# A refitted issue order and a refitted choice of masked tiles in an attention and FFN kernel

## The chip, the cores and the metric

The kernel runs on one core of a Trainium2 chip. A core has engines that run side by side, each with its own queue that it works off strictly in order: PE (matrix multiplication) with its weight loads (PEld), DVE (vector), ACT (activation), POOL (general), and SP, which here only issues transfers (DMA). The metric is the device time of one launch in microseconds. The kernel before takes 446.1 us, the median of three runs (445.67 to 448.51).

## The reference

Attention with a threshold, for 8 batches, 8 heads, 576 rows and a head size of 64, and after it an FFN over 4608 tokens with three parallel hidden layers (512 to 768) of which the largest value counts:

```python
scores = scale * np.matmul(q, k.transpose(0, 1, 3, 2))
thresh = np.max(scores, axis=-1, keepdims=True) - tau
scores = np.where(scores >= thresh, scores, -1e9)
attn = np.exp(scores - np.max(scores, axis=-1, keepdims=True))
attn = attn / (np.sum(attn, axis=-1, keepdims=True) + 1e-09)
x = np.matmul(attn, v)            # then heads side by side: 4608 x 512
h = np.maximum(np.maximum(x @ w1, x @ w2), x @ w3)
out = h @ w_out                   # 4608 x 512, float32
```

## The kernel before

A batch has two groups of four heads. Each group is nine chunks of 128 score rows; a chunk holds rows of two head pairs, r = 0 and 1, so a chunk has two score tiles of 128 x 576, 288 tiles in all. The last batch is done in two parts (four and five chunks for each group) so that its FFN can begin earlier.

The order of everything is written out by hand in one long string, ORDER. A loop at the end of the kernel reads it letter by letter, and each letter issues one step for the next item of its kind. Each engine is wrapped in `_Ordered`, which fixes its instructions in the order of the string, so the string decides the sequence in all queues. What one engine waits for from another follows from the data. Letters S, T, O and F carry a digit, the one of the four banks of PSUM that the step writes. A bank is free again when the engine that reads it is done.

The letters, by the engine that does the work:

- PE: S scores of a tile; T transposes q or k of a later group; O product of probabilities and v; F first half of an FFN product (hidden layer, tile ph, or output, tile po); B its second half.
- DVE: m the row maximum of a tile; k masks and sums a tile; r the reciprocals of a chunk's two sums; c copies transposed k; v maximum over the hidden layers (tiles hm, hT); w copies an attention output.
- ACT: e the first activation of a tile; n the second exponential with its sum; a copies transposed q; h copies the first hidden layer; x copies an attention output; u copies an FFN output.
- POOL: p scales a tile by its reciprocal (tile P); q swaps the halves of q (tile qs); y casts v; z casts weights.
- SP: l loads q, k and v of a later group; g loads weights (tile stage, 512 KB each); t transposes a chunk's P by DMA into ptq, which O reads; o stores results.

MASKED is a string of 288 bits, one for each score tile, and chooses between two ways to do its softmax. An unmasked tile (0) has its maximum on DVE, and then two activations on ACT: one that flattens all that lies below the threshold, and an exponential that sums (e and n). A masked tile (1) has its maximum on DVE, one exponential on ACT (e), and the threshold and the sum on DVE (k). So the bit moves work between ACT and DVE:

```python
def numerators(g, idx, r, zn, sm):
    acc = sm[:, r:r + 1]
    if masked(g, idx, r):
        vector.scalar_tensor_tensor(out=zn, in0=zn, scalar=thr, in1=zn,
                                    op0=OP.is_ge, op1=OP.mult, accum_out=acc)
    else:
        scalar.activation(out=zn, in_=zn, func=AF.Exp, scale=-1.0 / FLAT, accum_out=acc)
```

Buffers bind the engines to one another: four banks of PSUM, z tiles for four chunks, six P tiles, two stage tiles, two ptq. A prologue written as code (`beginning`) does the first group's q and k and the first two score tiles ahead of the string. Nearly all instructions are recorded at one line, that of the wrapper, so the profile is read by tile names.

Of the kernel before, what the change touches and what calls it, by code (L numbers as in the profile page):

```python
# [45 lines left out]
1eplBrkepF2tnmF3BnpvBnqvT1S0hprrcT2S3pamS1eymzF2emBeqgkF0etyS3nS1vpnmtF2pBmezBveS3prgnS0mtS1phrmT3epO2metzeF
0wpnS1gcqS2nmBqnmO3zekepgS1xvlF2nS3mtnF0rrmpBeBlpveS1lphS2mntF3zmeBrpS0evS1lpnmF2lnpS3rmleBptmS1nzvS0nS3mtpn
S2rpeF1rmepmtepS0mBepmtekF3ektekT2uBarklpukS0uqlS2urS1mlnS3pmleO0pmlepmelO2wtnkS1xrS0tepmF2myF3eBkepT1tBhcF0
nqvT2T1laByrcynS3qvS2nlqmF1tnpF0meS3pBelmBlhrrF2kpelS1vnBlprF3mnlS0pveBtprmS1hS2pmeS3tpmeS0pmF2emF1eBkeT3Bva
tF0nvqT2T3BkqlaS1nrcS3phmtS2npmF0epF1mteBqkBeqF3lnvS2lnBrvplS0hmtpS1F3meS2mteBrmepS0vnpO1rekpnO3mtnpweS2yrrt  # L50
xS1mF0yymT3epBcnS1pvS2nptF3meS0pmeBomT2hS1okeF0omF3ntBkaBervS1ponrF2vpemS0ptuS3mpeF2metknT1T3rknBparrceS0puS
3mqtuS1mpeS2mpeS3lmF0peomepS1ketqT3S2ncBqnmlqnmlO3ekluktO1urnwperrS0pxS3mptnS2mS1pempS3etmF0peF2meBlkBelS1kh
oF3nrmlF0pnBtvpBerrvS2phlS1mnpS3tmF0peS2mpeBmeF3vF1eoBkntS0vnBS2rmhpS3mepS1mteyF2mF0eyBkteBnrvT3pF1aovT2ynBp
lrcS3hplS0mnyF2lmF1elBykepBlnvT3tS0aS2vnO3rrmtpnmpeS1weptS2mS0prmO3eqtmeqF1eqlT0S2xqcBnlpmS3hlpS0meF2ymF1elB
knlF3vnBokBetS2hvS0nrrF3mpF1mpeBkBpetF2vnprS0uvnT3ptmS2aS1pmeS0trmF3epmnpkeS2tS0ermpBnmopnkS1uS2rurompS0eF3o
mpelmpeS2lkpeS0lmS1elqBmelqmetkO2unktO0erwpurkpT1txT2cS3apF0nmtT1qS2ceBqmnS1yF3hmF2eyrBpeBvptnF0pS1vnBrmtpS3
hS2pmeS0mtS1eF3meF2meBkBeF0knF1vnBBrvhpS3nvT0pF2akyF1tnBmyS0velByrmlS3phS2rlempF1lmyeF0pklBepS3tnvS2nBrmptO1
meprvepS2wnS3plmF0nF1rmepBlkeqS2lBhmtT3nyS0vnS2mqlO1emtpecT2xT0rS3pacF1eqmF2lnyBklqeT0BvlaS3khoS1qnmF0tF2pme
BrBopnvS3teprvF0pnrmS1puS2meS3prmS0epF1tmepmepT2ktBeqncT3tuS0kaS2urqmS3tnpmS1nF0pmemteS3repS1mS2lepmBelykteS
3kuO1rumplnmlpO0ewterpT2xS1cqnoS3mpF0nF2metBkeBkF1hlF3nvBlnrrS0pvlnBpmS2lhS1ymleF0mtS3epBmepF2vF1etkBnS0vnS3  # L60
rmBnpS2rhmpF0emF1pteBkpBerF3vnS2ptvnT0pBramS1pthS0mepF3meqtT2rBecpS1nvylT0ynS2pmlS3amlS1eomS0elO2rmpeomeplO3
ketnwT1F0nctF2xkBnBrvpS1hrF3pmS0qBemqS2onvF1yeF0mBopkeF3tyBnS2vqhBrlrnmpT1S0vaptS2empF1S3mpelBkeplF0vntS2rum
S1pnS0mtepF3rmepmetqS2kS0epBnmmteS1rkepS2lmuS0ulpmS1nlymT3yetF2cekeT3oBrknpamoS0npS3mnS1qtmuO0qurrmqelO2wpel
kpelS0xS3meptF2mS1peBemytF0hrkT3pBecF2nS1vpnS3rymtBpnmS0epS1vlnF3mF2etBmeBkhF0lkeF3nBrvpS1nrvBpnS2mptS0hmpeS
3meF2tmF1eBkeBlrvnT0plS3ravlpS2nlmqF0nlS1mqeBtrrmpF2eS3phBlmepS0tvepS1mS2npS3mepO0meknO1meownT3orxkT2pS0tacF
# [687 lines left out]
```

## Time and profile before

| | |
|---|---|
| median of 3 runs | 446.1 us (445.67 to 448.51) |
| the profiled execution | 446.82 us, span 445.0 us |
| PE busy | 423.6 us (95%) |
| ACT busy | 394.4 us (89%) |
| DVE busy | 393.2 us (88%) |
| POOL busy | 315.9 us (71%) |
| mean granted PE clock | 0.992 of full speed |

The span is the time from the first to the last instruction; the run's time has 1.8 us more around it. A share of busy time is a mean over the whole span, and the stages differ: the first FFN work can begin only when a batch's attention is done, and the last batch's FFN is left alone at the end. Matmuls are pipelined and their ends are modelled, so PE's gaps are seen better in the waits of its weight loads.

### The profile page before, as it was taken

The page shows a single profiled execution, that of the slowest core. Times are in us where ns is not written, and L with a number is a line of the kernel's source. Part 1 is how long each engine was busy: PE and PEld are TensorE (multiplying, and loading weights), DVE is VectorE, ACT ScalarE, POOL GpSimd, SP SyncE. Part 2 cuts the span into 40 slices and gives each one's busy share as a digit, 9 for nine tenths or more (in the row PEclk, how much of TensorE's full clock was granted, in tenths as well). Part 3 has the DMA queues.
Part 4 walks back from the last instruction along what each step waited for, and adds up shares of the span by engine and source line. Part 5 has one row for each costly group of instructions (what it writes and reads, how often), then busy time and mean ns, then how long its engine had stood idle before and what let it go on. Part 6 is the DMA issues. An engine that isn't in the chain of part 4 may idle for free.

```text
span 445.0 us, 14089 instructions
## 1 busy us (share of the span) xinstructions
PE 423.6 (95%) x5193; PEld 313.3 (70%) x5193; DVE 393.2 (88%) x1093; ACT 394.4 (89%) x804; POOL 315.9 (71%) x422
## 2 busy tenths in 40 slices
PE   7767799999999999999999999999999999999995
...
ACT  4999999999999999999998999999999999956422
...
GB/s 251 331 162 213 243 195 234 221 245 229 215 255 195 250 165 175 234 187 228 179 223 170 200 224 182 211 234 199 197 220 202 253 121 173 148 122 34 217 13 108
DMA packets 212773, 87.44 MB, mean 196 GB/s; under 512 B 185824, under 2 KB 199648, under 8 KB 212704
## 3 DMA queue, kind: packets, MB, share of 16 engines
...
q8 instruction: 41, 0.67, 0.6%
...
## 4 chain that ended last, share of the span: by engine, by line
PE 81%; ACT 7%; DVE 6%; issue 4%; POOL 2%; DMA 1%; DVEq 0%; POOLq 0%; ACTq 0%
PE ph L91 30%; PE sc L91 28%; PE po L91 11%; PE o L91 8%; ACT z L91 6%; PE tp L91 4%; DVE z L91 2%; DVE unused L91 2%; DMA qm<-in_q_dram 1%; POOL P L91 1%; DVE hm L91 0%; POOL w L91 0%; ACT qt L91 0%; POOL qs L91 0%; DVE hT L91 0%
## 5 line engine op out<-in xcount | busy, mean ns | idle before, releaser
L91 POOL TENSOR_SCALAR P<-z,rs 128x576 bf16<-128x576 f32 x288 | 228.1, 807 | 85.7 <-DVE rs L91 36.4
L91 PE MATMUL sc<-kt,qt 64*128 64x320 f32 (+2 forms) x640 | 179.1, 429 | 4.9 <-ACT z L91 4.4
L91 PE MATMUL sc<-kt,qs 64*128 64x256 f32 (+2 forms) x640 | 178.6, 418 | 4.7 <-ACT z L91 2.7
L91 PE MATMUL ph<-xt,w 64*128 64x288 bf16 (+2 forms) x2160 | 163.9, 283 | 0.3
L91 PEld LDWEIGHTS <-w 64*128 64x128 bf16 (+1 forms) x2160 | 124.8, 94 | 30.9 <-issue 5.3
L91 DVE TENSOR_SCALAR_CACHE_REDUCE unused<-sc 128x576 bf16<-128x576 f32 x183 | 133.2, 749 | 8.9 <-PE sc L91 8.4
L91 ACT ACTIVATE z<-sc,nm 128x576 f32<-128x576 f32 x183 | 131.3, 740 | 8.5 <-DVE unused L91 5.2
L91 ACT ACTIVATE z<-z 128x576 f32<-128x576 f32 x183 | 123.5, 680 | 0.1
L91 PEld LDWEIGHTS sc<-kt,qs 64*128 64x128 f32 (+1 forms) x640 | 92.4, 178 | 25.3 <-ACT z L91 8.1
L91 PEld LDWEIGHTS sc<-kt,qt 64*128 64x128 f32 (+1 forms) x640 | 92.4, 178 | 19.8 <-ACT z L91 9.3
L91 DVE SCALAR_TENSOR_TENSOR z<-z 128x576 f32<-128x576 f32 x105 | 84.1, 811 | 0.4 <-ACT z L91 0.4
L91 DVE TENSOR_SCALAR_CACHE_REDUCE z<-sc 128x576 f32<-128x576 f32 x105 | 77.7, 752 | 7.4 <-PE sc L91 3.4
L91 ACT ACTIVATE z<-z,nm 128x576 f32<-128x576 f32 x105 | 79.1, 773 | 3.6 <-DVE z L91 3.2
...
L91 PE MATMUL po<-wo,hT 64*128 64x512 bf16 (+1 forms) x480 | 54.0, 356 | 0.1
L91 DVE TENSOR_TENSOR hm<-ph,hm 128x576 bf16<-128x576 f32 (+2 forms) x54 | 37.0, 686 | 13.0 <-PE ph L91 11.8
L91 ACT ACTIVATE hm<-ph 128x576 bf16<-128x576 f32 (+2 forms) x54 | 32.1, 594 | 18.4 <-PE ph L91 18.1
L91 PEld LDWEIGHTS <-hT 64*128 64x128 bf16 (+1 forms) x480 | 29.6, 97 | 17.1 <-issue 2.9
L91 DVE TENSOR_TENSOR hT<-ph,hm 128x576 bf16<-128x576 f32 (+2 forms) x54 | 37.2, 688 | 3.1 <-PE ph L91 0.6
L91 PE MATMUL o<-ptq,vb 128*64 128x64 bf16 (+2 forms) x544 | 38.7, 282 | 0.0
L91 ACT ACTIVATION_READ_ACCUMULATOR z<-z 128x1 f32 x183 | 36.2, 198 | 0.0
L91 PEld LDWEIGHTS <-vb 128*64 128x64 bf16 x544 | 22.6, 111 | 15.1 <-issue 6.8
...
## 6 DMA issues: line engine op xcount, KB each, us to landing
...
```

What stands on the lines that cost most here:

```text
L91: ins = fn(*a, **kw)
```

## The change

The two strings are new; nothing else is. The text of ORDER has the same letters as before, but for three k that are n now, since MASKED has 102 ones instead of 105. Thirteen bits differ: tiles 74, 138, 149, 188 and 273 become masked, tiles 3, 151, 189, 268, 275, 277, 280 and 282 unmasked (counted from 0 in the order of the score tiles). In ORDER most lines differ, but the steps of one engine mostly keep their neighbours. The diff, with the masks whole and the first and last lines of the order:

```diff
 MASKED = """
-010100101001000000011101001010000001100010001000101000011000100000100000
-000011111001100001001001001001000001011100101001000110001010010000010011
-000010011101100001001100100001001010001100010111000001000100000110000101
-001001001101100000110001000100100100001100100011100111010011010111110110
+010000101001000000011101001010000001100010001000101000011000100000100000
+001011111001100001001001001001000001011100101001000110001010010000110011
+000011001101100001001100100001001010001100011011000001000100000110000101
+001001001101100000110001000100100100001100100011100101010110000101010110
 """
...
 ORDER = """
-lllllmlyelgS2ymylS3emgnlT0mleS1lakS2nlqermS3ylmeS0pmeS1kpS3elmS2nlzmelrmnT1pS0tcnperkT1pameS1zmteS3knpS0rnmp
-emS2permeqS1mnqT3meqktepS0ncS2ntrpmS3npretprmeS1pmnS0tpmS3npmS1etpmeS0rT2mnplkeT1akgeS2qmgepmteS3rkpekntS0pe
-rrnmT2pncS3ptamepS1meqtrS2meyqnS3lmqeS0pmelpknT1lpS2nmeymeS3lrkepS0tcnT2rpnmS1tpnmaprrmS0eS2pmteS1pmT3epctep
-meT3O0ykntnyS2etrykpnO1wnprmaS0xptrS3meS2zmeS1mzgeS0mlnS3pmleS1pmelO2qmelpkteO0nrnklpS3nlwgxprrmS2leS0pmeF3q
...
-0eF1kpteBnBvpF3BvtBrhkpF2S0vS1prmBptmF3eF0pveBtBhS1vS2mS3mF0F1mBkBF2vhF3keBeO0vnO1kF2kxeBwurS1rvpS0mpS2F3mpe
-tmpeS0eoF1mnketBknkBurrupoF2puF0hptF3uvF2pvF1hF0tvF3rvpF2hF1vopF0vF3thF2vF1vF0hoF3vF2ovF1hF0vF3vO2uoO1wF0xF3
-F2hF1vF3vF2hF1vF3vF2hF1vF3vF2hF1vF3vF2hF1vF3vF2hF1vBvF3uuooBF2uuuooo
+lgllmglyeS2mlnylS3mezlS0emlnkS2lermlpS1nmlT3palmeS3qreS1mpeS0mqT2nmS1ynclzerlmT2epS3kleplamS0ntS2pmS3nymetme
+qT1keqercS0nprkS2S1nptempnmS3teprrmepS0metS2pnS1pmntpS0nrmpnmtS2permT1peS3mgpekS2ngkalemS1qterkpeT0meptrkeT3
+pnS2mnpctS1arymnqS0emlqeS3ymqelkS1pelmntS2pmnS0rmetpmeS3perkT1peT2cnS0rptmS1npmnprtmS0nyT1armetS2peO3mpncpte
+kpT1ekeS0tyaS2rmnpO1nrpwepmtS3xS0zmeS2mnzS1gmepgmeS3lerkS0pleS1mO2nlpmelrmqnO3lkyelweptS0nS2pS1xlrmpnF3lmpet
...
+2kF1noBvBhkS0F3rrmpF2vBpeS0pvntF1mpnBBhroS3pevF2opmS0tS1meF3meBtBevS1hkF0F2mBeS3vBnmF1nrvO0pnO3pwkS2txeS0kF3
+morrmeopF2kpekBnptunrBupruptF0uF1phF3uvpF0tvF2phF1vF3tvF0hF2vF1voF3hF0vF2voF1hF3ovF0voF2hF1ovF3vO0uoO2wF1xF3
+F0hF2vF3vF0hF2vF3vF0hF2vF3vF0hF2vF3vF0hF2vF3vF0hF2vBvF3uuoBF0ouuuooo
 """
```

More of the change, by code (lines that the diff above doesn't have):

```diff
@@ L40 @@
 ORDER = """
-lllllmlyelgS2ymylS3emgnlT0mleS1lakS2nlqermS3ylmeS0pmeS1kpS3elmS2nlzmelrmnT1pS0tcnperkT1pameS1zmteS3knpS0rnmp
-emS2permeqS1mnqT3meqktepS0ncS2ntrpmS3npretprmeS1pmnS0tpmS3npmS1etpmeS0rT2mnplkeT1akgeS2qmgepmteS3rkpekntS0pe
-rrnmT2pncS3ptamepS1meqtrS2meyqnS3lmqeS0pmelpknT1lpS2nmeymeS3lrkepS0tcnT2rpnmS1tpnmaprrmS0eS2pmteS1pmT3epctep
-meT3O0ykntnyS2etrykpnO1wnprmaS0xptrS3meS2zmeS1mzgeS0mlnS3pmleS1pmelO2qmelpkteO0nrnklpS3nlwgxprrmS2leS0pmeF3q
-tmT1eBqcF0eqkthBpnS2vS1nF3pmnF0pmBerBkepS2vhT1tnprmS0S3apmetS1zmeS2rmpeF3tmF0epBkepF1tnBvBznvS2ghS3rymnF0gmS
@@ L46 @@
[L46 to L65, printed above, removed]
@@ L66 @@
-1nF2qrmeBtpS3evpBmS0tyhF1meT2yBcqoeF3rpkT2F0aptBnvBnS2pvS1hqtmF3nqT0meBrS1npvF2npmT3BactS1ervF3prmS0pueS2omp
-F3ekqelmT1ntS0qcnBpmekteS2S1urrmpF0uompekS3eptS2nmS1pnmlO3ermtpekO2pnwS1ykxtyS3emS2BomeyrmepS1rukpS2uoF3meF0
-opmnBtykBhpS1ervS2eptmO3pO0mxnS3txS2rmepF0empF1ekBtBevF3hkS2nS0mnBrmF1npF2vepBkBtS0hvO3emO2xkS1xerS3rpmF2mpF
-0eF1kpteBnBvpF3BvtBrhkpF2S0vS1prmBptmF3eF0pveBtBhS1vS2mS3mF0F1mBkBF2vhF3keBeO0vnO1kF2kxeBwurS1rvpS0mpS2F3mpe
-tmpeS0eoF1mnketBknkBurrupoF2puF0hptF3uvF2pvF1hF0tvF3rvpF2hF1vopF0vF3thF2vF1vF0hoF3vF2ovF1hF0vF3vO2uoO1wF0xF3
@@ new lines @@
+BrmpnF0kT1hpBtecS3nvS2qF1nmqF0ermqBeBkzteS3vhT2mS1npgS0raprmeS2pmeS3pmeF0zmF1nBknpgF2eBvtBpervS0hpS3tmnF1ymS
+2eBtymeF0yvnpF3BkntqBnvT2T1qhrrrtS0cazS3meS2mpegF1mlpeBS0lzevS3lnmF2pngF1mpBtekBpeS0vhS3tprmnT2S1pmeO0zmerce
+pF3gwnS2pS1nmqBnmqO0erkzevS2xS1mnpgF3mnlF0pBreptBvepS2rnF1tpmS3hzBemS0tnvpF2nS3mztBemS1pervS3eplS0mnF2plmnlr
+kpetS1meS3prmS0etpBmepmeF1tkekuT3nkBtakuS0kulS3urrS2mpnlS1pemlO0prmelymO3elweptkS2xpS0nmF1tF3mqeBkpeT2tBrhcF
+0pnvT1T2taBqrcnS3qvS1nlqmF2lF0ymyelS3pBelmBplhrkF1pelS2vnBtpF3mnS0prveBtprS2mhS1pmeS3pmeS0mpF1etmF2eBkeT3Blv
@@ new lines @@
+aF0nvqT1T3ntBcqaS2rkhS1qlmnS3tpmF0eF2mpeBklyBetF1vnS3rnvpBlS0mhqlS2meF1lpmS3etBrrmepS0vpO2eokpntO1mnpwnS3rxr
+pS2emF1pmT0etBycynS2yvF3ntS0mepBmeF1porkhS0poS2nmBonpmF3teS0rvyT2yeBkplaF1vtpS2mueS3mqF1etmqekT0nT3rBcnpekpS
+2aruS0mptuS3meqS1meS0pmF2etqmnS3rknpT0oBempecS1lkeS0umlO3urormnpokeO2pterwnpS1S0xlpmS3nlpmS2elF1mpetF0mBekBe
+S3lkhF2lnrmF1tpBnvpBerrvS0tphS3mynS2mF1epS0meBpmnF2tpvF3eBkeS1lvnBS0mhlS2rmepS3lmepF0tmF1eBkeBtvnF2rT3nvpT0B
+alrcpS1hS3pmtF0pmF2eBkyetT1BvaqS3nlvqS1nrO0mtpnmyeS2pwlnS3rmtS1pemO0epmelqkT2teqF1xS3cBnmlS0hrS2pmeF3pmF1eBk
@@ new lines @@
+teF0vnBrBkpS2hvS3npmF0nF1mtBekBerF2vopnrrS3ovupnT0mS2ptaS1mpeS3mF0petmpekS2etS1knBnrrmplmpS3luS2rpumlS1epmF0
+temqekS2tpeS1mS3epmBemtekO2nkluuO1klewllT0rxrpS3cT2pF1maT0nBtqcS2epS0mhF3qnrmF1qeBBpevF2nptS0vnBprmS3hptS1me
+S2pmS0elyF3meF1omyeBykByelF2vnF0lrknByBtvhyS3npvT2F1lpamF0rtBkepS2vnBpmS3hS1lemF0lmeF2orBkeptS3rnvS1pnBmlpnO
+0rvleplmlS2pnwS3oepmF1tmF0eBrkepS2ohBmoT3nqS1vntS2ymeO0mepcT2qxT1T3acS0qtF2maF1qerkBpleBvS3hF0kqtnS2mnF1mpBe
+BrvtepS3rrnpF0mlpvS2unS3mytS0eymS1peF2mpterkpeT3mBnycteS0kupT3oumS1aS2prmnlS0pmeS3lpemF1lnlmqleS0rplS3emBpte
@@ new lines @@
+mekS2lekO0ntrmpuO3uwperkpT1xS0cnS2qmtF3nF1mpeBkteBF0hrpF2nvtBpnS3vnqBrmtS1yhyS0myeF3mS2epBmeF1pvnF0tkBeS3nvB
+lnrmS2pS1hlmpF3emF0teBrkpeBvS2nlF1pnvlT3BrrtampS0hrpS3melF1mqetT2BqecS0npvT3nS2pmS1apmtS0empS3eO2mlermopeO1w
+lepknlqT0F2xlcF3nqrtkBnpBvS1htF0pmnS2S3etmBmF1eF2ovnBrkeBplF0rnrvS3phBmptT1S2vapS3meF0ptmS1eyBkepF2vnS3rtymu
+nS0ymS2eF1mpempeS3rketpS2mnBpmertkS0epS3umuS2qmoeT0F1mplncoeS3okeT0BrakpntmS2nqS0meS3lqrulkO2pulnmlO1pewtepm
+S2xrpS0etmF1pmS3eBrmepF2khT0qBecS1tnvF3pnS0myBtnmS2nrS1vpeF0ompF3emBeoBkhlF2keF0lrnBvplS1nrvpBlnS3mptS2hmpeS
```

4 lines of the change are left out of this document (added).

## The prediction

> **What bounds the kernel now.** I read the page's busy shares and slices first, then the chain of work that ended last, then the table by stage, then the waits of the long middle stage.
>
> ```profile
> span 445.0 us, 14089 instructions
> ...
> PE 423.6 (95%) x5193; PEld 313.3 (70%) x5193; DVE 393.2 (88%) x1093; ACT 394.4 (89%) x804; POOL 315.9 (71%) x422
> ...
> PE   7767799999999999999999999999999999999995
> ...
> ACT  4999999999999999999998999999999999956422
> ...
> PE 81%; ACT 7%; DVE 6%; issue 4%; POOL 2%; DMA 1%; DVEq 0%; POOLq 0%; ACTq 0%
> ```
>
> Three engines are above 87%, but not for the same length: PE is dense from the sixth slice to the end, ACT from the second slice to the thirty-fifth. The chain is 81% PE. So the kernel has a front in which ACT is the limit, a middle in which PE and ACT are both nearly full, and an end that PE alone sets. The table by stage, cut where PE becomes dense and where the last attention product begins, gives the sizes.
>
> ```profile
> core 0: us, PE busy (x) PEld busy (x) DVE busy (x) ACT busy (x) POOL busy (x), PEclk, DMA share, GB/s
> 0.00:20.00 20.00, 14.02 (x139) 9.91 (x139) 13.00 (x39) 14.06 (x29) 12.65 (x24) 1.00 0.93 294
> 20.00:65.00 45.00, 34.77 (x310) 21.46 (x312) 40.15 (x122) 43.79 (x92) 40.58 (x54) 0.92 1.07 208
> 65.00:380.00 315.00, 314.33 (x4020) 237.71 (x4016) 297.44 (x824) 303.29 (x619) 244.40 (x323) 1.00 1.02 208
> 380.00:422.70 42.70, 42.70 (x560) 33.11 (x562) 35.74 (x98) 27.67 (x56) 18.29 (x24) 1.00 0.71 123
> 422.70:445.00 22.30, 17.83 (x176) 11.13 (x172) 6.87 (x15) 5.61 (x12) 0.00 (x0) 0.99 0.17 60
> ```
>
> In 20 to 65 us ACT is idle for 45.00 - 43.79 = 1.21 us: nothing that a new order does there can win more, unless it takes work off ACT. In 65 to 380 us ACT is idle for 315.00 - 303.29 = 11.71 us and DVE for 17.56 us. PE shows 0.67 us idle, but its busy time is modelled; its real gaps are read from its weight loads, which wait for banks of PSUM:
>
> ```profile
> PEld L91 <- issue: 10.7, 31, 0.5
> ...
> ACT z L91 <- DVE unused L91: 4.6, 13, 0.7
> PEld sc L91 <- ACT z L91: 4.5, 17, 0.4
> PEld sc L91 <- issue: 4.5, 17, 0.4
> ...
> PEld sc L91 <- DVE z L91: 2.2, 7, 0.5
> PEld tp L91 <- ACT z L91: 2.1, 7, 0.5
> ...
> PEld sc L91 <- ACT qt L91: 1.1, 4, 0.4
> ...
> PEld sc L91 <- ACT hm L91: 1.0, 4, 0.5
> ```
>
> The rows that name another engine make 4.5 + 2.2 + 2.1 + 1.1 + 1.0 = 10.9 us in 315 us. None is longer than 0.5 us. That is all the middle has to give to a better order; the "issue" rows wait for nothing that the profile shows.
>
> **The change, part by part.** Nothing is added to or taken from the PE, POOL or SP work: both texts hold the same letters except three k (the masked sum on DVE) that become three n (the second exponential on ACT). Thirteen mask bits change, five to 1 and eight to 0.
>
> *The masks.* What a tile costs by either way:
>
> ```profile
> L91 ACT ACTIVATE z<-sc,nm 128x576 f32<-128x576 f32 x183 | 131.3, 740 | 8.5 <-DVE unused L91 5.2 <-POOL P L91 1.9 <-DVE rs L91 0.6
> L91 ACT ACTIVATE z<-z 128x576 f32<-128x576 f32 x183 | 123.5, 680 | 0.1
> L91 DVE SCALAR_TENSOR_TENSOR z<-z 128x576 f32<-128x576 f32 x105 | 84.1, 811 | 0.4 <-ACT z L91 0.4
> L91 ACT ACTIVATE z<-z,nm 128x576 f32<-128x576 f32 x105 | 79.1, 773 | 3.6 <-DVE z L91 3.2
> L91 ACT ACTIVATION_READ_ACCUMULATOR z<-z 128x1 f32 x183 | 36.2, 198 | 0.0
> ```
>
> By busy time an unmasked tile costs ACT (131.3 + 123.5 + 36.2) / 183 = 1.59 us and a masked one 79.1 / 105 = 0.75 us: 0.84 us apart. By starts it is less, since neighbours overlap:
>
> ```profile
> 385.65 0.69 ACT L91 ACTIVATE z<-z 128x576 f32<-128x576 f32 x1
> 386.22 0.21 ACT L91 ACTIVATION_READ_ACCUMULATOR z<-z 128x1 f32 x1
> 386.31 0.69 ACT L91 ACTIVATE z<-z 128x576 f32<-128x576 f32 x1
> ```
>
> The second exponential with its accumulator takes 386.31 - 385.65 = 0.66 us of ACT, and that is what an unmasked tile adds. So one flip moves 0.66 to 0.84 us onto ACT and takes 84.1 / 105 = 0.80 us from DVE. Counted along the tiles, ACT carries one tile more from tile 3 to tile 73 (the front and the start of the middle), is level to 137, carries one less (two for a few tiles) to 267, and ends three more, from four net flips among tiles 268 to 282.
> - Front: 0 us. The extra tile costs ACT 0.66 us where ACT is the limit, but ahead of the first F the new text holds 48 e against 49, so one activation of about that size (0.65 us by starts, 131.3 / 183 = 0.72 by busy time) falls out. Bounds: +0.84 if that one is late again, -1.21 if all of ACT's idle time goes.
> - Middle: -0.7 us. From tile 138 to 267 ACT has one tile less, where ACT is busy for 303.29 of 315 us and DVE, which takes it, for 297.44. Bounds 0 (PE alone is the limit) and -0.84.
> - End: 0 us. Four tiles put 2.6 to 3.4 us on ACT. The cover is ACT's 42.70 - 27.67 = 15.03 us of idle time in 380 to 422.7 us while PE is busy throughout. With the cover gone it would cost those 3.4 us.
>
> *Loads and first transposes.* Two 512 KB weight loads now stand on SP's queue ahead of the second group's large q and k loads; all later SP entries of that stretch stand behind them.
>
> ```profile
> 7.02 0.47 SPq L91 DMA_DIRECT2D qm<-in_q_dram  x1
> 7.53 0.48 SPq L91 DMA_DIRECT2D km<-in_k_dram  x1
> ...
> 10.04 0.59 SPq L91 DMA_DIRECT2D stage<-in_moe_w_dram  x1
> ```
>
> At the 294 GB/s of the first 20 us, 1.05 MB take 3.6 us, so q and k come up to 3.6 us later. The transposes that read them move back too: the first from after the 4th score tile to after the 7th. Three tiles at ACT's pace (0.72 + 0.66 us for an unmasked one) are about 4 us, which covers the 3.6. In return the last swap of that group is issued after the 15th tile instead of the 17th, well ahead of its first reader, the 19th. I take 0; bounds 0 and +3.6.
>
> *The rest of the order.* On PE 138 of 712 steps have another place in the sequence, 105 of them by one, none by more than 7. On ACT and DVE about seven in ten move, mostly by one or two. On POOL and SP the moves are by 2 on average (P, its DMA transpose, loads and stores). Counted at each 24th score tile, PE's own queue holds the same steps ahead of it but for one or two. Steps that only trade neighbours can change the 10.9 us of bank waits and no PE work. From what the trace shows both signs are open: -10.9 at most; upward, the nearest row is ACT's wait for DVE's maxima, 4.6 us in 13 times, 0.35 us each, and three times as many would cost 9.2. I take 0, the value between, since most steps keep their neighbours.
>
> *The tail.* The order behind the last O differs in bank numbers and in the place of one store only. Ahead of it the last DMA transpose stands farther off:
>
> ```profile
> 418.69 1.31 SPq L91 DMA_TRANSPOSE ptq<-P  x1
> ...
> 422.73 0.60 PE L91 MATMUL o<-ptq,vb 128*64 128x256 bf16 x8
> ```
>
> Now 4.0 us lie between; the new text puts 12 F between them instead of 8. PE did not wait there, so this is 0, and safety against a late landing.
>
> *Sum.* 0 - 0.7 + 0 + 0 + 0 = -0.7 us. The profiled execution took 446.82 us (445.0 span, 1.8 around it), 0.7 over the median of the runs, 446.1, and inside their spread. So 446.8 - 0.7 = 446.1 for that execution, and 446.1 - 0.7 = 445.4 for the median: **445.4 us, no change that can be told.** 1% is 4.5 us, about what a measurement of this kernel can tell from nothing.
>
> **The rivals.**
> *A, the refit finds the waits (faster).* If half of the 10.9 us of bank waits go, with the 1.2 us of the front and the 0.7 of the masks: 446.1 - 5.5 - 1.2 - 0.7 = 438.7; with a third of the waits 440.6. For it: the waits are many and short, the sort that a fit in small steps can reach. Against it: ACT has only 11.7 us idle there, so a gain of 5.5 asks ACT for 98% over 315 us. 0.17.
>
> *B, DVE's maxima come late (slower).* Place: 65 to 380 us, on ACT's first activation of a tile, which waits for DVE's maximum; behind it stand ACT's next exponentials, and PE waits for the bank that they free. Price 0.35 us each. From 15 more such waits on, about twice the present number, the change is over 1% slower (15 x 0.35 - 0.7 = 4.5); three times the number gives 446.1 + 9.2 - 0.7 = 454.6, and a middle course of 20 more gives 452.4. For it: some seven in ten steps of both engines have moved, and DVE has one tile more to do from 138 to 267. Against it: the moves are of one place. 0.25.
>
> *C, the clock falls (slower).* The trace shows PE's granted clock below 1 in one stretch:
>
> ```profile
> 30.00:40.00 10.00, 7.45 (x69) 3.89 (x68) 9.54 (x30) 10.00 (x23) 8.97 (x12) 0.92 1.12 212
> 40.00:50.00 10.00, 6.95 (x52) 4.72 (x50) 9.09 (x29) 9.52 (x22) 9.54 (x14) 0.84 1.01 241
> 50.00:60.00 10.00, 9.08 (x94) 6.42 (x96) 7.73 (x22) 9.39 (x19) 8.77 (x13) 0.90 1.21 196
> ...
> PEld sc L91 <- ACT z L91: 11.3, 13, 2.2
> ```
>
> That is (0.08 + 0.16 + 0.10) x 10 = 3.4 us of full-speed time lost, hidden there behind ACT. The same loss inside the dense stage, twice, would give 446.1 + 6.8 - 0.7 = 452.2. Against it: that stage has waits of 0.5 us at most and a clock of 1.00 for 315 us. 0.03.
>
> The Trainium skill, TensorE: Matmul & The Clock Gate, section HAM oscillation, puts the fall at idle gaps of more than about 3.4 us. By that rule there would be no fall at all in this kernel, and C would be nothing. The trace disagrees: the longest wait for a bank in that stretch is 2.2 us and the clock fell. The same page's section on psum-queue depth-cycling, many small gaps between groups, agrees with the 13 waits, which is why C keeps a small chance.
>
> *D, it does nothing.* The old and the new order cost the same everywhere, the masks too: 446.1. 0.10.
>
> **How the numbers follow.** Forecast 0.45, D 0.10, together 0.55 within 1%. A gives 0.17 faster by more than 1%; B and C 0.28 slower. The range goes from 440 (a little beyond A's third) to 453 (B with 20 more waits, and C): about 0.07 lie below and 0.11 above.
>
> **What would show it.** Front: PE's first hidden-layer matmul (67.5 us now) stays within 1 us; q and k land before their transposes. Middle: ACT busy about 302 to 303 us in 65 to 380; the rows of PE's bank waits sum to 8 to 14 us, ACT's waits for DVE to 3 to 8 us. A shows as bank waits under 6 us, B as ACT waits for maxima over 9 us, C as a PEclk digit under 9 behind 65 us. The end: PE unbroken from 390 us, ACT busier by some 3 us behind 380 us. I am wrong if PE stands still for more than 1 us at once anywhere behind 65 us, for data of a DMA say, which the present trace never shows.

## The result and the profile after

The changed kernel takes **448.14 us** (median of 20 runs, 447.31 to 449.54) against 446.21 us for the kernel before (20 runs, 445.49 to 448.51). The ratio is 1.0041 with a 95% interval of [1.0029, 1.0053]: 1.9 us slower, where the forecast was 0.7 us faster. That is inside the range and within 1%, but on the wrong side of zero. The profiled execution took 447.87 us with a span of 446.1 us.

The page of the changed kernel: busy shares, ACT's slices, the chain that ended last.

```profile
span 446.1 us, 14115 instructions
...
PE 426.0 (95%) x5193; PEld 308.6 (69%) x5193; DVE 394.3 (88%) x1087; ACT 395.4 (89%) x810; POOL 316.8 (71%) x422
...
ACT  4999999999998999999898999999999999877522
...
PE 77%; ACT 8%; DVE 6%; issue 4%; POOL 3%; DMA 1%; SPq 0%; POOLq 0%; DVEq 0%; ACTq 0%
```

PE's share of the chain fell from 81% to 77%, and ACT's end is denser (8775 instead of 9564 in slices 35 to 38). Only the chain says that PE waits more; the busy sums hardly do. The table by stage of the changed kernel, with the same columns as before:

```profile
core 0: us, PE busy (x) PEld busy (x) DVE busy (x) ACT busy (x) POOL busy (x), PEclk, DMA share, GB/s
0.00:20.00 20.00, 15.03 (x140) 10.62 (x141) 12.62 (x38) 14.20 (x30) 12.38 (x25) 1.00 0.93 281
20.00:65.00 45.00, 35.25 (x318) 19.27 (x316) 41.16 (x124) 43.97 (x95) 40.64 (x53) 0.96 1.07 221
65.00:380.00 315.00, 314.12 (x4004) 233.93 (x4002) 298.98 (x822) 300.37 (x612) 243.43 (x320) 1.00 1.03 203
380.00:423.75 43.75, 43.75 (x568) 33.67 (x566) 34.72 (x92) 31.24 (x66) 20.34 (x27) 1.00 0.74 139
423.75:446.10 22.35, 17.84 (x176) 11.13 (x172) 6.88 (x15) 5.61 (x12) 0.00 (x0) 1.00 0.21 77
```

The middle is where the work thins out: 4004 matmuls fell into the same 315 us instead of 4020. The stage from 380 us is 1 us longer, with ACT 3.6 us busier (31.24 against 27.67) as the four unmasked tiles there ask. The tail is 22.35 us against 22.30. The waits of the middle, 65 to 380 us, changed kernel (engine and tile that wait, who is waited for: sum, times, longest):

```profile
PEld sc L91 <- ACT z L91: 4.1, 15, 0.4
...
PEld sc L91 <- DVE hT L91: 2.5, 7, 0.6
ACT z L91 <- DVE z L91: 2.5, 5, 0.9
PEld sc L91 <- ACT qt L91: 2.2, 6, 0.6
ACT z L91 <- DVE unused L91: 2.1, 5, 0.7
PEld sc L91 <- DVE z L91: 2.0, 7, 0.5
PEld tp L91 <- ACT z L91: 2.0, 7, 0.5
PEld sc L91 <- ACT hm L91: 1.6, 6, 0.5
```

Two of these rows were small in the same window of the kernel before:

```profile
PEld sc L91 <- DVE hT L91: 0.9, 3, 0.4
...
ACT z L91 <- DVE z L91: 0.6, 3, 0.2
```

They are new among the large ones: score tiles wait for DVE's maximum over the hidden layers (hT 2.5 us; 0.9 before), and ACT waits for DVE's z (2.5 us; 0.6 before), with 0.9 us at once. All rows of score tiles and transposes that wait for DVE or ACT, small ones too, sum to 17.2 us before (13.7 and 3.5) and to 19.1 us after (15.5 and 3.6): 1.9 us more, the size of the loss. The prediction's 10.9 us had only the five rows that it showed.

One group of DVE is costlier per instruction than before. It is the masked sum, step k; the groups of DVE between 65 and 385 us, first of the kernel before, then of the changed one (count, busy us, mean ns):

```profile
L91 DVE SCALAR_TENSOR_TENSOR z<-z 128x576 f32<-128x576 f32 x80 | 63.6, 804 | 0.0
```

```profile
L91 DVE SCALAR_TENSOR_TENSOR z<-z 128x576 f32<-128x576 f32 x79 | 64.8, 831 | 0.1
```

One sum fewer takes 1.2 us more. A mean that moves with neither shape nor type may point at single slow instances, and the timeline shows them. The changed kernel from 136 to 141 us, DVE and then POOL (start, us, engine, work):

```profile
136.92 0.75 DVE L91 TENSOR_SCALAR_CACHE_REDUCE unused<-sc 128x576 bf16<-128x576 f32 x1
...
138.28 1.66 DVE L91 SCALAR_TENSOR_TENSOR z<-z 128x576 f32<-128x576 f32 x1
...
139.87 0.75 DVE L91 TENSOR_TENSOR hm<-ph,hm 128x576 bf16<-128x576 f32 x1
```

```profile
136.88 1.47 POOL L91 TENSOR_SCALAR P<-z,rs 128x576 bf16<-128x576 f32 x2
138.29 1.04 POOL L91 CAST vb<-vm 128x1024 bf16<-128x1024 f32 x1
```

A sum that takes 0.75 us alone took 1.66 us. It ended at 139.94, 0.61 us after POOL's cast of v ended (138.29 + 1.04 = 139.33). The cast began with the sum, 0.01 us after it, when the P tiles ahead of it still ran for 0.06 us. DVE's maximum at 136.92 ran beside a POOL instruction without loss, so it is not every DVE instruction. The profile counts the standing still as busy time of DVE, and there is no wait row for it. What it does to others is seen in the waits of 136 to 143 us of the same kernel:

```profile
ACT z L91 <- DVE z L91: 0.9, 1, 0.9
PEld sc L91 <- DVE hT L91: 0.6, 1, 0.6
...
PEld sc L91 <- DVE hm L91: 0.4, 1, 0.4
```

### The profile page after: what moved, and what is told of

Read it like the earlier page. It is cut to its first block, busy times and chain, and to the rows that moved or that the text cites. A ratio compares the mean times of both kernels' runs of the same rounds, so it can differ in the third digit from the quotient of the medians.

```text
span 446.1 us, 14115 instructions
## 1 busy us (share of the span) xinstructions
PE 426.0 (95%) x5193; PEld 308.6 (69%) x5193; DVE 394.3 (88%) x1087; ACT 395.4 (89%) x810; POOL 316.8 (71%) x422
## 4 chain that ended last, share of the span: by engine, by line
PE 77%; ACT 8%; DVE 6%; issue 4%; POOL 3%; DMA 1%; SPq 0%; POOLq 0%; DVEq 0%; ACTq 0%
PE ph L91 29%; PE sc L91 27%; PE po L91 9%; PE o L91 8%; ACT z L91 7%; PE tp L91 3%; DVE z L91 3%; DVE unused L91 2%; POOL P L91 1%; POOL qs L91 1%; PE warm L91 1%; ACT qt L91 1%; DMA out_dram<-ob 1%; DVE hT L91 0%; POOL vb L91 0%
## 5 line engine op out<-in xcount | busy, mean ns | idle before, releaser
L91 PE MATMUL ph<-xt,w 64*128 64x288 bf16 (+2 forms) x2160 | 165.8, 283 | 0.2
L91 DVE TENSOR_SCALAR_CACHE_REDUCE unused<-sc 128x576 bf16<-128x576 f32 x186 | 135.5, 750 | 8.7 <-PE sc L91 7.7
L91 ACT ACTIVATE z<-sc,nm 128x576 f32<-128x576 f32 x186 | 133.9, 750 | 8.6 <-DVE unused L91 3.6
L91 ACT ACTIVATE z<-z 128x576 f32<-128x576 f32 x186 | 126.8, 690 | 0.2
L91 PEld LDWEIGHTS sc<-kt,qs 64*128 64x128 f32 (+1 forms) x640 | 90.9, 177 | 26.8 <-ACT z L91 7.8
L91 PEld LDWEIGHTS sc<-kt,qt 64*128 64x128 f32 (+1 forms) x640 | 91.0, 177 | 22.1 <-ACT z L91 7.2
L91 DVE TENSOR_SCALAR_CACHE_REDUCE z<-sc 128x576 f32<-128x576 f32 x102 | 75.8, 752 | 7.1 <-PE sc L91 4.5
L91 PEld LDWEIGHTS <-hT 64*128 64x128 bf16 (+1 forms) x480 | 28.1, 97 | 18.1 <-issue 2.6
L91 ACT ACTIVATION_READ_ACCUMULATOR z<-z 128x1 f32 x186 | 38.7, 208 | 0.0
```

What stands on the lines that cost most here:

```text
L91: ins = fn(*a, **kw)
```

## The experiments

All are made from the two kernels' own strings. Each is timed against the kernel before on the same chip; that kernel's median lay between 446.50 and 447.04 us there (446.21 beside the changed kernel), so ratios compare better than times. Beside the times I use PE's gaps: for each PE step (S, T, O, F, B) the time from its start to the next step's start, less the lower quartile of that time for steps of its kind over all these kernels. Summed by PE work done, the gaps show where an order loses. Up to 90 us of PE work they vary from profile to profile without an edit (a1_add below has 1.7 us more at 30 to 90 than the kernel before, with the same order there). Behind 105 us, the kernel before, h1_front, h4_end, a1_add and b1_ports, which share their order there, agree to 0.04 us in each stretch of 15 us where none has an edit; h5_front83 has the same order behind its seam and differs in two stretches, by 0.42 and 0.26 us, and by up to 0.1 us in a third, which I did not follow up. Gaps in us, columns by stretch of PE work in us:

```
              0-30   30-90  90-225  225-315  315-390 | 90-390  less before
before       26.55    4.80    7.07     4.25     1.67 |  12.99
after        25.52    4.70    8.27     4.25     2.54 |  15.06     +2.07
h1_front     25.78    5.93    6.85     4.28     1.67 |  12.80     -0.19
h5_front83   26.71    5.64    7.25     4.59     1.67 |  13.51     +0.53
h2_rest      25.48    5.39    8.52     4.14     2.76 |  15.41     +2.42
h4_end       25.74    5.18    7.04     4.24     2.07 |  13.35     +0.36
m1_masks     25.89    5.26    9.94     4.50     1.67 |  16.12     +3.14
m2_order     25.74    5.40    9.01     4.33     2.54 |  15.87     +2.89
w1_casts     26.22    4.87    6.84     4.25     2.06 |  13.16     +0.17
a1_add       26.26    6.52    7.27     4.24     1.67 |  13.17     +0.19
b1_ports     26.86    5.51    6.88     4.24     1.67 |  12.80     -0.19
best2        25.72    4.69    6.72     4.26     2.35 |  13.34     +0.35
best3        26.19    4.68    6.72     4.25     3.47 |  14.44     +1.46
```

The changed kernel's +2.07 us behind 90 us is about the size of its +1.93 us of time: 1.20 at 90 to 225 us of PE work, nothing to 315, 0.87 in the rest.

**Where in the order: four splices.** h1_front has the new order and mask up to the first F, the old behind it; h5_front83 the new order to the 83rd score tile, the old behind; h2_rest the old order to the first F, the new behind; h4_end the old order to the 265th score tile, the new behind (with banks 0 and 1 exchanged, as the seam asks). The masks go with the order. For h1_front and h4_end, with the first lines that differ:

```diff
-010100101001000000011101001010000001100010001000101000011000100000100000
+010000101001000000011101001010000001100010001000101000011000100000100000
...
-lllllmlyelgS2ymylS3emgnlT0mleS1lakS2nlqermS3ylmeS0pmeS1kpS3elmS2nlzmelrmnT1pS0tcnperkT1pameS1zmteS3knpS0rnmp
+lgllmglyeS2mlnylS3mezlS0emlnkS2lermlpS1nmlT3palmeS3qreS1mpeS0mqT2nmS1ynclzerlmT2epS3kleplamS0ntS2pmS3nymetme
...
```

```diff
-001001001101100000110001000100100100001100100011100111010011010111110110
+001001001101100000110001000100100100001100100011100101010110000101010110
...
-F3ekqelmT1ntS0qcnBpmekteS2S1urrmpF0uompekS3eptS2nmS1pnmlO3ermtpekO2pnwS1ykxtyS3emS2BomeyrmepS1rukpS2uoF3meF0
+F3ekqelmT1ntS0qcnBpmekteS2S1urrmpF0uompekS3eptS2nmS1pnmlO3ermtpekO2wnkS3xS1emS2prmBeptmeyF3rkpuS2uS1nmpF0tem
...
```

> The new order and tile 3's mask up to the first F, the old order and masks behind it. In the two profiles the first hidden-layer matmul starts 1.5 us earlier in the changed kernel, and the end comes 1.1 us later. Theory L (local: what a stretch of the order wins or loses stays in the total): 446.2 - 1.5 = 444.7, at least 1 us faster than before. Rival G (given back: the middle is held by ACT's and DVE's work, not by when PE's FFN work begins): 446.2, as before.

> The other half: the old order up to the first F, the new order and masks behind it. Theory L: the changed kernel's 448.1 without the front's gain, 448.1 + 1.5 = 449.6. Rival G: the front is worth nothing either way, 448.1, as the changed kernel.

> The old order and masks up to the 265th score tile, the new ones behind it. In the profiles the changed kernel falls back by 0.7 us between 364 and 380 us, and by nothing afterwards. Theory L: 446.2 + 0.7 = 446.9. Rival: the fall is a late effect of the middle's order (ACT and DVE arrive there late), and the end alone costs nothing, 446.2.

> The new order and masks up to the 83rd score tile, where both orders have issued all but one of the same steps, the old ones behind it. The cut at the first F left a seam: PE stood idle for 2.9 us in the 15 us of PE work behind it, where both whole orders show 1.8. Theory L (a stretch keeps what it wins, the first cut lost 1.1 us at its seam): 446.3 - 0.6 = 445.7, and no seam. Rival G (the front's gain is given back whatever the cut): 446.3 to 446.8.

Measured: h1_front 447.27 us, ratio 1.0011 [0.9997, 1.0026]; h2_rest 449.88, 1.0083 [1.0060, 1.0106]; h4_end 447.25, 1.0015 [1.0001, 1.0030] (the kernel before beside these three: 446.50); h5_front83 448.20, 1.0022 [1.0003, 1.0041] (beside 446.94).

The new front is not faster. In the profiles of the two kernels the first hidden-layer matmul starts at 67.54 us before and at 66.06 after, which looked like a gain of 1.5 us that something later gives back. Over all these kernels the old front brings it at 66.7 to 67.8 us and the new one at 66.1 to 67.4 (means 67.2 and 66.6), and the gaps of the first 30 us have means of 26.13 (six kernels with the old front) and 25.98 (seven with the new). So nothing is given back; there was no gain that can be told. h2_rest comes out at theory L's 449.6, but not for its reason: by the same theory h1_front should have taken 444.7. The new end costs little: h4_end has 0.40 us more gaps behind 315 us of PE work. The splices themselves aren't free: at 30 to 45 us, where their seam lies, h1_front has 2.89 and h2_rest 2.74 us of gaps, and the other eleven kernels 1.76 to 1.83. So they place the loss only roughly: some in the middle, some at the end, none in front.

**Is it the masks or the order?** m1_masks is the kernel before with the six flips of the middle alone, two e moved by one and two places; m2_order is the changed kernel with five flips undone.

```diff
-000011111001100001001001001001000001011100101001000110001010010000010011
-000010011101100001001100100001001010001100010111000001000100000110000101
+001011111001100001001001001001000001011100101001000110001010010000110011
+000011001101100001001100100001001010001100011011000001000100000110000101
...
-knlF3vnBokBetS2hvS0nrrF3mpF1mpeBkBpetF2vnprS0uvnT3ptmS2aS1pmeS0trmF3epmnpkeS2tS0ermpBnmopnkS1uS2rurompS0eF3o
+knlF3vnBokBetS2hvS0nrrF3mpF1mpeBkBpetF2vnprS0uvnT3ptmS2aS1pmeS0trmF3epmnpkeS2teS0rmpBkmopnnS1uS2rurompS0eF3o
...
```

```diff
-001011111001100001001001001001000001011100101001000110001010010000110011
-000011001101100001001100100001001010001100011011000001000100000110000101
+001011111001100001001001001001000001011100101001000110001010010000010011
+000010011101100001001100100001001010001100010111000001000100000110000101
...
-mekS2lekO0ntrmpuO3uwperkpT1xS0cnS2qmtF3nF1mpeBkteBF0hrpF2nvtBpnS3vnqBrmtS1yhyS0myeF3mS2epBmeF1pvnF0tkBeS3nvB
+mekS2lenO0ktrmpuO3uwperkpT1xS0cnS2qmtF3nF1mpeBkteBF0hrpF2nvtBpnS3vnqBrmtS1yhyS0myeF3mS2epBmeF1pvnF0tkBeS3nvB
...
```

> The old order, with the six mask flips of tiles 74 to 189 alone (two activations stand one or two places earlier so that their bank is read in time). The prediction's term for them: ACT has one tile less from 138 to 267, -0.7 us, 445.5. Rival P (PE alone is the limit there): 446.2. Rival V (DVE's maxima become late as DVE has a tile more): above 446.7.

> The changed kernel with five of the six middle masks (tiles 138, 149, 151, 188, 189) put back. These flips cost the old order some 4 us. Theory F (masks and order are fitted to one another, either without the other loses): about 3 us slower than the changed kernel, 451. Rival M (these masks cost wherever they stand, and they are why the changed kernel is slower): faster than the changed kernel, down to 446.

Measured: m1_masks 450.66 us, ratio 1.0096 [1.0074, 1.0118]; m2_order 449.22, 1.0049 [1.0033, 1.0065]. Each half alone is slower than before, and m2_order isn't faster than the whole change. The flips aren't worth the 0.7 us that I gave them: in the old order they cost 3.1 us of gaps behind 90 us of PE work, 2.9 of them before 225, and undoing five of them in the new order adds 0.8 (in one profile; the ratios of m2_order and of the whole change overlap, and the 3 us that theory F asked for did not come). So the flips need a fitted order, as m1_masks shows; that the new order needs the flips is only likely. Rival V, late maxima, is not what m1_masks shows either: from 65 to 380 us ACT's waits for unmasked tiles' maxima fall from 4.6 to 3.8 us, while the score tiles' waits for ACT rise from 4.5 to 7.2 us, about the loss there. The stage of 190 to 230 us shows how, kernel before first, m1_masks below, with a wait of m1_masks between 208 and 216 us:

```profile
190.00:230.00 40.00, 40.00 (x508) 29.98 (x502) 37.45 (x106) 37.92 (x79) 31.05 (x42) 1.00 1.00 206
```

```profile
190.00:230.00 40.00, 39.18 (x494) 28.64 (x490) 36.50 (x102) 36.19 (x74) 30.61 (x41) 1.00 1.01 201
```

```profile
PEld sc L91 <- ACT z L91: 1.3, 1, 1.3
```

ACT is 1.73 us less busy there, and PE did 14 matmuls fewer. With second exponentials at other tiles, ACT comes late for one bank by 1.3 us there (score tile 153, behind the flips of 149 and 151), and it is idle elsewhere. Work taken off ACT returned nothing by itself.

**Do DVE's masked sum and POOL shut each other out?** w1_casts is the changed kernel with five casts of v on POOL written later, behind the next P tiles. No other step is moved, and the masks stay. Its lines that differ:

```diff
-aF0nvqT1T3ntBcqaS2rkhS1qlmnS3tpmF0eF2mpeBklyBetF1vnS3rnvpBlS0mhqlS2meF1lpmS3etBrrmepS0vpO2eokpntO1mnpwnS3rxr
+aF0nvqT1T3ntBcqaS2rkhS1qlmnS3tpmF0eF2mpeBklBetF1vnS3rnvpBlS0mhqlS2meF1lpymS3etBrrmepS0vpO2eokpntO1mnpwnS3rxr
...
-S2pmS0elyF3meF1omyeBykByelF2vnF0lrknByBtvhyS3npvT2F1lpamF0rtBkepS2vnBpmS3hS1lemF0lmeF2orBkeptS3rnvS1pnBmlpnO
+S2pmS0elyF3meF1omyeBykBelF2vnF0lrknBBtvhS3npyvT2F1lpamF0rtBkepS2vnBpyymS3hS1lemF0lmeF2orBkeptS3rnvS1pnBmlpnO
...
-0nmopekpT3tS1ecS2nmBqkepS3muF1urtrmpekpS0eS2nmS3ptmeO0pmetrkO2npwnkS3yxS0emS2prmBeptmeyF3rkpuS2uS0nmpF1temBp
+0nmopekpT3tS1ecS2nmBqkepS3muF1urtrmpekpS0eS2nmS3ptmeO0pmetrkO2npwnkS3xS0emS2pyrmBeptmeyF3rkpuS2uS0nmpF1temBp
```

> The changed kernel with five casts of v on POOL moved behind later P tiles, so that the masked sums on DVE at 138.3, 231.5 and 373.4 us (1.66, 1.34 and 1.58 us where an undisturbed one takes 0.75) no longer start while a cast runs. Theory W (a masked sum on DVE and a POOL instruction shut each other out, and the new order has them meet at worse places): 0.9 + 0.3 + 0.8 = 2.0 us of DVE time come back and at least 1 us of the total, 447.0 or less. Rival: these sums are not on the path, 448.1.

Measured: 447.15 us, ratio 1.0007 [0.9990, 1.0023] (beside 446.94), where the change as it is has 1.0041 [1.0029, 1.0053]; the two intervals do not overlap. The gaps behind 90 us of PE work fall by 1.90 us, from 15.06 to 13.16. In w1_casts the same sum, on DVE between 136 and 141 us, runs alone and takes its 0.75 us, and the group's mean from 65 to 385 us is back at 804 ns:

```profile
139.05 0.75 DVE L91 SCALAR_TENSOR_TENSOR z<-z 128x576 f32<-128x576 f32 x1
```

```profile
L91 DVE SCALAR_TENSOR_TENSOR z<-z 128x576 f32<-128x576 f32 x80 | 63.5, 804 | 0.0
```

ACT's wait of 0.9 us and the score tile's of 0.6 us are gone from 136 to 143 us, and the gaps of that stretch (90 to 105 us of PE work) fall from 1.53 to 0.67, less than the 0.93 of the kernel before. The second dear one stands near the end. The changed kernel between 371.5 and 376 us, DVE and POOL:

```profile
373.38 1.58 DVE L91 SCALAR_TENSOR_TENSOR z<-z 128x576 f32<-128x576 f32 x1
```

```profile
373.35 0.28 POOL L91 CAST vr<-vr 64x128 bf16<-64x128 f32 x1
373.62 0.74 POOL L91 TENSOR_SCALAR P<-z,rs 128x576 bf16<-128x576 f32 x1
```

Two POOL instructions back to back held it, and it ended 0.60 us after the second (374.96 against 374.36). In w1_casts it takes 0.78 us, and the gaps of 315 to 330 us of PE work fall from 1.18 to 0.71. A third sum, at 231.48 us, took 1.34 us beside a cast and takes 0.76 in w1_casts; PE stays in step there until 234 us and is 0.25 us ahead at 235.6. At 243.8 us it gains another 0.33 us, which nothing here assigns to one step.

Moving a cast frees the sum, but it also lets the P tiles behind the cast start earlier. The waits tell the two apart. From 136 to 143 us and from 371 to 378 us no row of the changed kernel waits for a P tile or for a transfer, and the rows that shrink are waits for DVE. In the second of these stretches the reciprocals stand behind the sum on DVE; the changed kernel and then w1_casts:

```profile
ACT z L91 <- DVE rs L91: 0.9, 1, 0.9
```

```profile
ACT z L91 <- DVE rs L91: 0.3, 1, 0.3
```

So the collision is shown as the cause of most of the loss: it was taken away by moving nothing but POOL's casts, the time went with it, and in the two dear places the waits that went are those for DVE. For the 0.25 and 0.33 us near 235 and 244 us it is likely and not shown.

The Trainium skill, SBUF — State Buffer, section Who interferes with whom, states just this: a VectorE instruction with two inputs in SBUF contends with a GpSimd instruction that reads SBUF, and the one issued first makes the other stand still. The trace agrees for the sum (both inputs are z): 1.66 us beside a cast, 0.75 us alone. It differs in one thing: POOL's next instruction can go ahead of a sum that already waits. The P tile that starts at 373.62 us did so, the cast at 138.29 us too by these starts, and a run below shows three more.

**Can the collision be put in?** a1_add is the kernel before with one cast of v written earlier, so that it runs when the masked sum at 139.56 us comes:

```diff
-tF0nvqT2T3BkqlaS1nrcS3phmtS2npmF0epF1mteBqkBeqF3lnvS2lnBrvplS0hmtpS1F3meS2mteBrmepS0vnpO1rekpnO3mtnpweS2yrrt
+tF0nvqT2T3BkqlaS1nrcS3phmtS2npmF0eypF1mteBqkBeqF3lnvS2lnBrvplS0hmtpS1F3meS2mteBrmepS0vnpO1rekpnO3mtnpweS2rrt
```

> The kernel before with one cast of v on GpSimd (1.04 us, at 147.4 us) written earlier, ahead of the score tile's work at 138.9 us, so that it is running when the masked sum at 139.56 us comes; nothing else is moved. If a collision of the masked sum with a cast is by itself what costs, where a tile's maximum over the hidden layers stands behind the sum on VectorE: the sum goes from 0.75 to between 1.0 and 1.7 us, and TensorE's gaps between 90 and 105 us of its work go from 0.93 to between 1.1 and 1.8 us; the time rises by 0.2 to 0.9 us, ratio 1.0004 to 1.002. Rival (what the run with moved casts won was not the sum but the score tiles' scaling and its transfers, which moved with the casts): the sum is stretched, the gaps there stay at 0.8 to 1.05, ratio 0.9995 to 1.0005.

Measured: 447.11 us, ratio 1.0001 [0.9984, 1.0018], the kernel before 447.04. The sum, which is at 141.01 us in this profile, grew to 0.97 us only, since the cast was nearly done. DVE and POOL of a1_add:

```profile
141.01 0.97 DVE L91 SCALAR_TENSOR_TENSOR z<-z 128x576 f32<-128x576 f32 x1
```

```profile
140.34 1.04 POOL L91 CAST vb<-vm 128x1024 bf16<-128x1024 f32 x1
141.35 1.25 POOL L91 TENSOR_SCALAR P<-z,rs 128x576 bf16<-128x576 f32 x1
```

The dose was small and so was the effect: 0.22 us more in the sum, 0.18 us more gaps at 90 to 105 us of PE work (1.11 against 0.93), nothing that the times could show. It has the sign and the place of the theory, but the time alone cannot tell the two apart. In return the P tile at 141.35 was held up by the sum (1.25 instead of 0.74 us).

**Does each such collision cost what it stretches?** b1_ports takes two collisions out of the kernel before, by moving a weight cast (z) behind the next P and a cast of v (y) behind the next:

```diff
-0wpnS1gcqS2nmBqnmO3zekepgS1xvlF2nS3mtnF0rrmpBeBlpveS1lphS2mntF3zmeBrpS0evS1lpnmF2lnpS3rmleBptmS1nzvS0nS3mtpn
+0wpnS1gcqS2nmBqnmO3ekepzgS1xvlF2nS3mtnF0rrmpBeBlpveS1lphS2mntF3zmeBrpS0evS1lpnmF2lnpS3rmleBptmS1nzvS0nS3mtpn
...
-hS2pmeS0mtS1eF3meF2meBkBeF0knF1vnBBrvhpS3nvT0pF2akyF1tnBmyS0velByrmlS3phS2rlempF1lmyeF0pklBepS3tnvS2nBrmptO1
+hS2pmeS0mtS1eF3meF2meBkBeF0knF1vnBBrvhpS3nvT0pF2akyF1tnBmyS0velByrmlS3phS2rlempF1lmeF0pklBepS3tnvS2nBrmpytO1
```

> The kernel before, its own order and masks, with two casts on GpSimd written later: a weight cast that stood ahead of a masked sum near 97 us, and a cast of a feature tile that stood ahead of one near 240 us, each now behind the next score tile's work. Theory W (VectorE's masked sum and a GpSimd instruction shut each other out, so that a cast which lands on a sum costs the path about what the sum is stretched): the two sums fall from 1.2 to 1.5 us to about 0.75, TensorE's gaps behind the front fall from 18.1 to 17.5 to 17.8, time 0.3 to 0.6 below the kernel before, ratio 0.9987 to 0.9993. Rival (the stretch lies beside other work here, and it cost something only in the changed order): the sums get shorter, the gaps and the time stay, ratio 0.9995 to 1.0005.

Measured: 447.57 us, ratio 1.0017 [0.9999, 1.0036], the kernel before 446.68. Neither expectation fits: the time doesn't fall, and the gaps do not stay. The sums did get shorter. At 97 us, DVE of the kernel before and then of b1_ports:

```profile
97.06 1.39 DVE L91 SCALAR_TENSOR_TENSOR z<-z 128x576 f32<-128x576 f32 x1
```

```profile
97.32 0.84 DVE L91 SCALAR_TENSOR_TENSOR z<-z 128x576 f32<-128x576 f32 x1
```

Of these 0.55 us PE got nothing: its steps stood 0.26 us behind those of the kernel before ahead of the sum and 0.27 us behind for 18 us after it. The sum at 240 us went from 1.16 to 0.76 us, and PE gained 0.16 us (the gaps of 195 to 210 us of PE work, 1.16 to 1.00). So the strong form of my theory falls: a stretched sum costs what it is stretched only where a bank that PE wants next stands close behind it on DVE, as at 138 us; elsewhere it costs part of that or nothing.

What stands against that gain in b1_ports is a product that waited 0.72 us for a transfer, at 75 to 90 us of PE work, and another queue explains it. The waits of SP between 92 and 100 us, kernel before and then b1_ports:

```profile
SPq L91 <- POOL wo L91: 0.4, 1, 0.4
```

```profile
SPq L91 <- POOL wo L91: 1.6, 1, 1.6
```

The weight cast frees a stage tile. Cast later, it held the next weight load, and with it SP's whole queue, 1.2 us longer. Five DMA transposes further on ended at 116.33 us instead of 114.92, and the attention product that reads them stood still. SP and PE of b1_ports:

```profile
107.38 8.95 SPq L91 DMA_TRANSPOSE ptq<-P  x5
```

```profile
116.45 0.40 PE L91 MATMUL o<-ptq,vb 128*64 128x512 bf16 x1
117.20 1.12 PE L91 MATMUL o<-ptq,vb 128*64 128x512 bf16 x14 [0.35 <-DMA ptq<-P]
```

That O took 2.18 us from its first to its last matmul's end instead of 1.42. The chain from the cast to the late product is in the trace step by step, but it is one profile: in a1_add, with no edit there, the same product came 0.5 us late too, behind a later queue of SP. That the edit caused it is therefore likely and not shown.

**What is left: the end, or a seam?** best2 is w1_casts up to the 265th score tile, with two more casts near 155 us moved, and the order and masks of the kernel before behind it (banks 0 and 1 exchanged):

```diff
-001001001101100000110001000100100100001100100011100101010110000101010110
+001001001101100000110001000100100100001100100011100111010011010111110110
...
-pS2emF1pmT0etBycynS2yvF3ntS0mepBmeF1porkhS0poS2nmBonpmF3teS0rvyT2yeBkplaF1vtpS2mueS3mqF1etmqekT0nT3rBcnpekpS
+pS2emF1pmT0etBycynS2yvF3ntS0mepBmeF1porkhS0poS2nmBonpmF3teS0rvT2eBkplaF1vtpyyS2mueS3mqF1etmqekT0nT3rBcnpekpS
...
-0nmopekpT3tS1ecS2nmBqkepS3muF1urtrmpekpS0eS2nmS3ptmeO0pmetrkO2npwnkS3xS0emS2pyrmBeptmeyF3rkpuS2uS0nmpF1temBp
+0nmopekpT3tS1ecS2nmBqkepS3muF1urtrmpekpS0eS2nmS3ptmeO0pmetrkO2npyoopnwS0ykxtyS3emS2BomeyrmepS0rukpS2uoF3meF1
...
```

> The changed kernel with its five casts of feature tiles and two more casts near 155 us moved behind the following score tile's work up to the 265th score tile, and from there the order and masks of the kernel before. Theory W with the end as a separate loss: the gaps behind the front are 18.3 (the run with moved casts) less 0.3 to 0.4 (the end), 17.9 to 18.0, so the time is that of the kernel before, ratio 0.9990 to 1.0000. Rival (what remained after the casts were moved is not the end but the seam of any two orders): the new seam costs as much as the end did or more, gaps 18.3 to 19, ratio 1.0005 to 1.002.

Measured: 447.33 us, ratio 1.0017 [1.0001, 1.0032]; gaps behind 90 us of PE work +0.35. The rival seemed to hold: behind 315 us best2 has 2.35 us of gaps, more than the 2.06 of the new end in w1_casts. But the loss sits in one stretch (315 to 330 us of PE work, 1.08 against 0.40), and there the splice had made a collision of its own. DVE of best2:

```profile
372.28 1.58 DVE L91 SCALAR_TENSOR_TENSOR z<-z 128x576 f32<-128x576 f32 x1
```

best3 moves the small cast that stands before it behind the next P:

```diff
-0nmopekpT3tS1ecS2nmBqkepS3muF1urtrmpekpS0eS2nmS3ptmeO0pmetrkO2npyoopnwS0ykxtyS3emS2BomeyrmepS0rukpS2uoF3meF1
+0nmopekpT3tS1ecS2nmBqkepS3muF1urtrmpekpS0eS2nmS3ptmeO0pmetrkO2npoopynwS0ykxtyS3emS2BomeyrmepS0rukpS2uoF3meF1
```

> The spliced kernel best2 with one small cast of v near 372 us moved behind the next score tile's work; in best2 the masked sum at 372.28 us took 1.58 us beside it. If that collision, made by the splice, is what the splice lost: the sum takes about 0.8 us, the gaps at 315 to 390 us of TensorE's work fall from 2.35 to between 1.7 and 2.0, those behind the front from 18.05 to 17.4 to 17.7 (17.81 in the kernel before), and the time is 0.3 to 0.6 us below best2's and at or 0.1 to 0.4 us under the kernel before's, ratio 0.999 to 1.0005. Rival (a splice costs there whatever stands beside it): the gaps stay at 18.0 or more, ratio 1.0005 to 1.002.

Measured: 448.46 us, ratio 1.0037 [1.0018, 1.0056], the kernel before 447.04: by its median slower than best2, not faster. The sum at 372.6 us did fall to 0.78 us. But the casts behind it moved too, and the next sum ran into them and into what follows. DVE, POOL and a wait of best3 between 375.5 and 382 us:

```profile
375.78 2.83 DVE L91 SCALAR_TENSOR_TENSOR z<-z 128x576 f32<-128x576 f32 x1
```

```profile
375.55 0.29 POOL L91 CAST vr<-vr 64x128 bf16<-64x128 f32 x1
375.82 2.18 POOL L91 TENSOR_SCALAR P<-z,rs 128x576 bf16<-128x576 f32 x3
```

```profile
PEld sc L91 <- DVE z L91: 1.3, 2, 0.9
```

A cast and three P tiles went ahead of the sum, back to back, and it ended 0.61 us after the last (378.61 against 378.00). Score tiles waited for it, and the gaps behind 315 us of PE work rose by 1.12 us (2.35 to 3.47) for one small cast moved by one tile. Unwanted as it was, this is the dose that a1_add lacked: 2.08 us more in a sum, about 1 us more in the gaps, and a ratio 0.0020 higher, though the two intervals still overlap.

Up to 315 us, behind 90, best2 and best3 have 10.98 us of gaps and the kernel before 11.32: without the collisions the new order is level with the old one or 0.3 us better, which these runs cannot tell. I have no version that beats both.

## Why the prediction was wrong, and where it was right

**The step that failed is "the rest of the order", taken as 0** between -10.9 and +9.2. It cost 1.2 us in the middle and 0.9 at the end (gaps), and most of that is one mechanism: casts of v that now start with or just ahead of a masked sum. w1_casts brought 1.90 us of the 2.07 back. I looked at the order's effect only through the bank waits that the waits view names. The old trace had the answer in another place: in the kernel before, too, the sum's mean of 811 ns is a mix of 0.75 us alone and more beside POOL, 1.39 us at 97 us for one. Such collisions are common, beside P tiles and copies as well as casts: 18 of that kernel's 105 sums took over 0.85 us, 28 of the changed kernel's 102. What the new order changed for the worse is where the longest of them stand. Without the collisions that w1_casts takes away, 0.17 us of gaps over the kernel before are left, so the forecast -0.7 us did not come even then. Of two engines that work at 88% and 71% I asked what waits for what, and not what they share. That most steps keep their neighbours on their own engine says nothing about what stands beside a step on another engine.

**The second step that failed is the masks of the middle, -0.7 us.** It counted ACT's busy time as if it were the path. m1_masks shows that flips without a fitted order cost: 3.1 us of gaps. ACT's busy time did fall in the middle, by 2.92 us (303.29 to 300.37): two net flips to masked lie inside that stage (74, 138, 149 and 188 against 151 and 189), 1.3 to 1.7 us at the prediction's price for a tile, and seven ACT steps fewer fell into it. The time did not follow; PE's waits for banks set it.

**The end, 0 us, with cover of 15.03 us**: nearly right. ACT got 3.6 us more in the stage from 380 us, and PE stayed full there (43.75 of 43.75 us). But the new end costs about 0.4 us of gaps all the same (h4_end 2.07 against 1.67, and w1_casts 2.06). A mean idle time of a stage isn't cover for each of its steps.

**Right**: the front at 0 (most of the difference in its one profile is gone when all profiles are taken, and no splice gains time); loads and first transposes at 0 (from 5 to 60 us PE waits 0.7 us for q and k by DMA, 1.1 before; of the two weight loads only one stands ahead of the large q load, both ahead of k); the tail at 0. Its last attention product does not wait in the changed kernel either:

```profile
423.79 0.60 PE L91 MATMUL o<-ptq,vb 128*64 128x256 bf16 x8
```

**The rivals.** A (half or a third of the waits gone) did not happen; the bank waits rose. B had the engine and the stage, DVE late in the middle, but not the mechanism: ACT's waits for maxima fell from 4.6 to 2.1 us, and the wait that rose is for the masked z, 0.6 to 2.5. B's price of 0.35 us in 15 more waits was too much; what came was two or three waits of 0.5 to 0.9 us. C did not happen: the clock is 1.00 behind 65 us. D, nothing, was nearest in size, but the interval excludes it: the prediction took 1% as about the least that a measurement can tell, and 20 runs of each kernel told 0.4%. Of the signs named, the first hidden-layer matmul moved by 1.48 us and not by under 1, most of it chance by the other profiles; ACT's busy time missed 302 to 303 by 2 us; the five rows of bank waits (4.1 + 2.0 + 2.0 + 2.2 + 1.6 = 11.9 us) and ACT's waits for DVE (2.1 + 2.5) stayed inside what I called right, so those bounds were too wide to see 1.9 us, and the rows left out (hT above all) held the sign.

What stays open: the 0.4 us of the new end in h4_end, whose step I did not look for; and why POOL's next instruction sometimes goes ahead of a sum that already waits (373.62, 375.82) and sometimes is held by it (the P tile after the cast at 97 us, which took 1.24 us).
